# The first two blocks of a fused attention and feed-forward kernel, issued by single steps in a listed order, with attention values gathered by TensorE

## The chip, the cores and the metric

One core of one Trainium2 chip. The time is the device time of one execution in microseconds (us). The kernel before took 239.2 us (median of 3 runs, 238.63 to 239.22). All runs told of here are of one core. Each run also lists its span (from the first to the last instruction) and the mean clock that PE was granted (1.0 is full speed). PE is TensorE, DVE VectorE, ACT ScalarE, POOL GpSimd, SP the engine that only issues transfers.

## The reference, cut to what matters

Chunked attention, then a gated feed-forward layer on its output.

```python
# q, k, v: (4, 8, 768, 64); mem_k, mem_v: (4, 8, 8, 64); chunks of 32 queries
for c in range(24):
    keys   = concat(mem_k, k[l_start:r_end])      # 8 memory rows, 16 left, 32 own, 8 right
    values = concat(mem_v, v[l_start:r_end])
    out[chunk] = softmax(q_c @ keys.T / 8) @ values
x = out as (3072, 512)
return (relu(x @ w_gate) * (x @ w_val)) @ w_out   # 512 -> 1536 -> 512
```

## The kernel before

The 3072 tokens are worked in eight blocks of 384. A block is four windows of 96 queries; eight heads make four head pairs (hp). For a head pair the steps are: turn (bring keys and queries to the layout with 64 dims on partitions), scores, exp, sums (denominators), values, and the product that gives x. A block's feed-forward part is twelve units m, each four matmuls for the gate, four for the value, a relu on ACT and a product on DVE; then three output tiles of twelve matmuls.

From block 2 on, each block's attention runs among the units of the block before it. Blocks 0 and 1 have nothing to hide behind: their order is written out by hand, in whole steps (cut, and short lines joined):

```python
    wide_v(0, 0); wide_d(0, 2); wide_v(0, 1)
    ...                                      # transfers, cut
    ffn_open(0, (0, 1)); wide_v(0, 2); wide_d(0, 3); chunk(0, 0); chunk(0, 1); wide_v(0, 3); chunk(0, 2); chunk(0, 3)
    ffn_close(0)
    ...
    ffn_unit(0, 2, spare=True); ffn_unit(0, 3)
    for hp in range(2):
        turn_pe(1, hp); turn_copy(1, hp)
    step_s(1, 0)                             # scores and exp
    for hp in range(2, HP):
        turn_pe(1, hp); turn_copy(1, hp)
    step_s(1, 1); wide_d(1, 0); ffn_unit(0, 4)   # wide_d: sums, then Ln and Exp
    step_s(1, 2); wide_d(1, 1); ffn_unit(0, 5)
    step_s(1, 3); wide_d(1, 2); ffn_unit(0, 6); wide_d(1, 3); ffn_unit(0, 7)
    one_words(0, ...); ffn_unit(0, 8); ffn_unit(0, 9)
    for hp in range(HP):
        wide_v(1, hp)
    one_words(0, ...); ffn_unit(0, 10); one_words(0, ...); ffn_unit(0, 11); one_words(0, ...)
    load_band(2, v, vwins); load_mem_v(2)
```

The value windows of all blocks come by `load_band`: four transfers a block, in rows of 64 elements. Block 1's units then run in a loop that also clears buffers on DVE, one piece after each of its first six units:

```python
    clear = [lambda: one_words(1, 0, 128, 0, NQ, ONE),
             lambda: (one_words(1, 96, 128, NQ - 1, NQ, 0), one_words(1, 96, 120, NQ - 1, NQ, ONE))]
    clear += [lambda p=p, hh=hh: clear_q(p, hh) for p in range(2) for hh in range(2)]
    ...
            if n == 2 and u < len(clear):    # u: the unit's number
                clear[u]()
```

The softmax here doesn't subtract the row's maximum and nothing guards it: scores larger than these inputs give would overflow.

## Time and profile before

| stretch | us | what limits it |
|---|---|---|
| start to block 1's first unit | 0 to 42.83 | waits among all engines and transfers |
| block 1's units | 42.83 to 63.47 | PE, without a gap |
| the rest | 63.47 to 237.0 | PE, without a gap up to the last output |

This is who PE waited for up to 43 us: writer and line of the waiting group, what ended the wait, us in total, times, longest.

```profile
PE xo_ps L297 <- DVE xT L299: 1.8, 3, 0.7
PE xo_ps L389 <- DVE filler L402: 1.3, 1, 1.3
PE kq_ps L199 <- DMA rq<-in_q_dram: 1.3, 1, 1.3
PE v_ps L342 <- DMA wv<-in_moe_w_val_dram: 0.8, 1, 0.8
PE xs_ps L285 <- ACT rw L288: 0.7, 1, 0.7
PE sc_ps L242 <- DVE kq L216: 0.7, 1, 0.7
PE kq_ps L199 <- POOL sel L429: 0.6, 1, 0.6
PE sc_ps L242 <- ACT ex L273: 0.3, 1, 0.3
```

The second line is the start of the program. The other seven make 6.1 us, and no engine stands out: four name DVE or ACT, two a transfer, one POOL. That is the picture of a start in which every engine hands on to the next. The table by stages and the chain are in the prediction.

### The profile page before, as it was taken

The page shows a single profiled execution, that of the slowest core. Times are in us where ns is not written, and L with a number is a line of the kernel's source. Part 1 is how long each engine was busy: PE and PEld are TensorE (multiplying, and loading weights), DVE is VectorE, ACT ScalarE, POOL GpSimd, SP SyncE. Part 2 cuts the span into 40 slices and gives each one's busy share as a digit, 9 for nine tenths or more (in the row PEclk, how much of TensorE's full clock was granted, in tenths as well). Part 3 has the DMA queues.
Part 4 walks back from the last instruction along what each step waited for, and adds up shares of the span by engine and source line. Part 5 has one row for each costly group of instructions (what it writes and reads, how often), then busy time and mean ns, then how long its engine had stood idle before and what let it go on. Part 6 is the DMA issues. An engine that isn't in the chain of part 4 may idle for free.

```text
span 237.0 us, 4591 instructions
## 1 busy us (share of the span) xinstructions
PE 225.4 (95%) x1730; PEld 131.6 (56%) x1730; DVE 107.4 (45%) x215; ACT 141.0 (59%) x299; POOL 103.8 (44%) x131
## 2 busy tenths in 40 slices
PE   6769888999999999999999999999999999999993
PEld 3535545566544566546664666556654666455641
DVE  5654727889720155604652156405551266214400
ACT  3393593367752589728883599538881798433310
POOL 7978967945306950991079402990040000000000
PEclk9999999999999999999999999999999999999999
DMA  7999999999994999499919998899902100120012
GB/s 120 136 177 194 196 173 184 153 186 161 133 144 178 138 168 173 29 170 163 156 20 145 151 148 87 54 190 150 135 0 89 44 3 0 44 91 0 1 46 89
DMA packets 107324, 27.35 MB, mean 115 GB/s; under 512 B 91222, under 2 KB 104358, under 8 KB 107302
## 3 DMA queue, kind: packets, MB, share of 16 engines
q0 software_dynamic: 83008, 15.37, 82.3%
q1 hardware_dynamic: 20630, 5.33, 19.4%
q10 hardware_dynamic: 3664, 6.36, 7.9%
q8 instruction: 13, 0.21, 0.4%
q14 instruction: 9, 0.07, 0.1%
HBM read 31.15 MB, written 6.29 MB: 158 GB/s over the span
## 4 chain that ended last, share of the span: by engine, by line
PE 85%; DMA 4%; POOL 3%; ACT 3%; DVE 2%; issue 1%; POOLq 0%; DVEq 0%; ACTq 0%
PE g_ps L342 25%; PE v_ps L342 25%; PE o_ps L368 25%; DMA wv<-in_moe_w_val_dram 3%; PE sc_ps L267 3%; PE xo_ps L306 2%; ACT ex L273 2%; PE xs_ps L306 2%; POOL vwin L142 2%; PE kq_ps L199 1%; DMA out_dram<-o_sb 1%; PE sc_ps L242 1%; POOL rk L127 1%; PE gv_ps L342 1%; ACT rw L288 0%
## 5 line engine op out<-in xcount | busy, mean ns | idle before, releaser
L349 DVE TENSOR_TENSOR gv<-v_ps,gr 128x384 f16<-128x384 f32 x95 | 52.8, 557 | 97.4 <-ACT gr L348 84.2
L342 PE MATMUL v_ps<-xT,wv 128*128 128x384 f16 x380 | 78.3, 326 | 0.8 <-DMA wv<-in_moe_w_val_dram 0.8
L342 PE MATMUL g_ps<-xT,wg 128*128 128x384 f16 x380 | 78.3, 326 | 0.0
L368 PE MATMUL o_ps<-wo,gv 128*128 128x512 f16 x288 | 63.5, 379 | 0.0
L348 ACT ACTIVATE gr<-g_ps 128x384 f16<-128x384 f32 x95 | 46.0, 486 | 22.0 <-PE g_ps L342 10.8
L342 PEld LDWEIGHTS <-wg 128*128 128x128 f16 x384 | 36.6, 98 | 22.7
L342 PEld LDWEIGHTS <-wv 128*128 128x128 f16 x384 | 36.2, 98 | 22.8 <-DMA wv<-in_moe_w_val_dram 1.0
L368 PEld LDWEIGHTS <-gv 128*128 128x128 f16 x288 | 28.1, 98 | 32.9
L230 POOL COPY qbd<-qT 64x1536 f16<-64x1536 f16 x10 | 14.6, 1462 | 58.5 <-DMA qT<-q16n 58.2
L377 ACT COPY o_sb<-o_ps 128x512 f32<-128x512 f32 x23 | 13.5, 586 | 39.0 <-PE o_ps L368 31.0
L273 ACT ACTIVATE ex<-sc_ps,bias 128x256 f16<-128x256 f32 x84 | 33.3, 467 | 3.9 <-PE sc_ps L242 3.2
L142 POOL DMA_DIRECT2D vwin<-in_v_dram x32 | 29.0, 934 | 1.7 <-DMA memv<-in_mem_v_dram 1.3
L315 ACT ACTIVATE rinv<-ln,mln 64x768 f32<-64x768 f32 x24 | 22.1, 923 | 0.0
L310 ACT ACTIVATE ln<-xo_ps 64x384 f32<-64x384 f32 x24 | 11.7, 487 | 16.3 <-PE xs_ps L306 16.3
L168 POOL DMA_DIRECT2D q16n<-in_q_dram x20 | 15.6, 805 | 5.5 <-DMA wo<-in_moe_w_out_dram 5.5
L142 POOL DMA_DIRECT2D k<-in_k_dram x20 | 17.9, 909 | 0.0
L321 DVE TENSOR_TENSOR xT<-xo_ps,rinv 64x384 f16<-64x384 f32 x24 | 13.1, 547 | 10.1 <-ACT rinv L315 10.0
L321 DVE TENSOR_TENSOR xT<-xs_ps,rinv 64x384 f16<-64x384 f32 x24 | 13.2, 550 | 0.7
L306 PEld LDWEIGHTS <-vwin 128*128 128x128 f16 x192 | 10.6, 98 | 3.0
L310 ACT ACTIVATE ln<-xs_ps 64x384 f32<-64x384 f32 x24 | 11.4, 474 | 0.0
L306 PE MATMUL xo_ps<-ex,vwin 128*128 128x96 f16 x96 | 11.1, 206 | 0.0
L306 PE MATMUL xs_ps<-ex,vwin 128*128 128x96 f16 x96 | 11.1, 206 | 0.0
(79 smaller groups left out, 134.9 us busy)
## 6 DMA issues: line engine op xcount, KB each, us to landing
out_dram<-o_sb ACTq DMA_DIRECT2D x23, 256.0 KB
vwin<-in_v_dram POOLq DMA_DIRECT2D x24, 120.0 KB, 7.5
q16n<-in_q_dram POOLq DMA_DIRECT2D x20, 96.0 KB, 5.5
k<-in_k_dram POOLq DMA_DIRECT2D x15, 120.0 KB, 4.6
wg<-in_moe_w_gate_dram POOLq DMA_DIRECT2D x6, 256.0 KB, 7.7
wv<-in_moe_w_val_dram POOLq DMA_DIRECT2D x6, 256.0 KB, 8.3
wo<-in_moe_w_out_dram POOLq DMA_DIRECT2D x3, 512.0 KB, 9.7
rk<-in_k_dram POOLq DMA_DIRECT2D x5, 224.0 KB, 7.0
```

What stands on the lines that cost most here:

```text
L142: pool_dma(dsts[p][NMEM + m0:NMEM + m1, i, :, 0:D], src)
L168: pool_dma(q16s[n][:, i], src)
L230: nc.gpsimd.tensor_copy(qbds[n % 2][s, :, :, hh, :].rearrange("p i a m -> p (i a) m"), qTs[n][s].rearrange("p i a m -> p (i a) m"))
L273: nc.scalar.activation(flat[:, :, :, s], view[:, :, :, s], ACT.Exp, scale=SCALE, bias=bias[:, g:g + 1])
L306: nc.tensor.matmul((xo, xs)[hh][:, QB * i:QB * i + QB], lhsT=vw[:, i, 2 * hp + hh, :], rhs=ex[:, hh, i, :], start=True, stop=True)
L310: nc.scalar.activation(ln[:, hh], (xo, xs)[hh][D:128], ACT.Ln, scale=1.0 / 64.0)
L315: nc.scalar.activation(rinv, lns.pop((n, hp)), ACT.Exp, scale=-1.0, bias=mln64[0:D, :])
L321: nc.vector.tensor_tensor(out=x_of(n)[D * hh:D * hh + D, hp, :], in0=(xo, xs)[hh][0:D], in1=rinv[:, hh, :], op=ALU.mult)
L342: nc.tensor.matmul(ps[a], lhsT=(wg, wv)[a][:, f, 128 * m:128 * m + 128], rhs=xTs[n][:, f, :], start=(f == 0), stop=(f == NFC - 1))
L348: nc.scalar.activation(gr, g_ps, ACT.Relu)
L349: nc.vector.tensor_tensor(out=gvs[n][:, m, :], in0=v_ps, in1=gr, op=ALU.mult)
L368: nc.tensor.matmul(o_ps, lhsT=gvs[n][:, m, 128 * t:128 * t + 128], rhs=wo[:, m, :], start=(m == 0), stop=(m == NDC - 1))
```

## The change

Its intent: cut PE's waits before block 1. Three parts, in the words of its author: blocks 0 and 1 by single steps in an order found with a model of the engines, values gathered by TensorE, block 2's memory values sent while block 0's units run.

The order is now a list of short names (T turn, S scores, e exp, D sums, L and E the Ln and the Exp of the denominators, G gather of values, cg its copy, V values, m product, g and v the halves of a unit, r its relu, mu its product):

```diff
-    ffn_unit(0, 2, spare=True)
-    ffn_unit(0, 3)
-    for hp in range(2):
-        turn_pe(1, hp)
-        turn_copy(1, hp)
-    step_s(1, 0)
...
+    go("""
+        Vb1 mb0 Vb3 Vb2 mb1 ch0 Eb3 ch1 mb2 mb3 ch2 ch3 r0 r1 g2 v2 mu0 r2 T0 mu1 g3 cq0 v3 ck0 T2 r3 mu2 mu3
+    """)
+    zero(vwins[0][0:NMEM + 16, 0, :, 0:D], 0.0)
+    load_mem_v(2)
+    go("""
+        cq2 ck2 T1 ck1 S0 g4 e0 cq1 v4 r4 S1 D0 mu4 T3 e1 L0 g6 S2 e2 v6 ck3 D1 cq3 r6 E0 g5 mu6 L1 r5 S3 v5 g7
+        v7 mu5 e3 r7 g9 mu7 E1 D2 G0 r9 g8 v9 L2 cg0 mu9 v8 G1 D3 cg1 E2 r8 g11 V0 v11 L3 r11 mu8 m0 V1 g10 m1
+        V2 m2 V3 E3 m3 v10 mu11 r10 mu10
+    """)
```

The values of blocks 0 and 1 come in rows of 256 elements and are spread to windows by a selection matrix on PE; the key order inside a window changes with it (masks and biases too):

```diff
-    load_band(0, v, vwins)
+    load_rows_mem(pool_dma, rv[KR:KR + 2], 0, 0, H, mem_v)
+    load_v_rows(0)
...
+    def gather_v(n, g, pool, tag):
+        ps = vgs[n, g] = pool.tile([128, 2, 512], F32, tag=tag, name="vg_ps").rearrange("p a (i c) -> p (a i) c", i=2)
+        for i in range(NQ):
+            for j in range(J):
+                nc.tensor.matmul(ps[32 * j:32 * j + 32, i].rearrange("p (h d) -> p h d", d=D),
+                                 lhsT=sels[n][0:KR + 2, i, :], rhs=rv[:, 4 * g:4 * g + 4, D * j:D * j + D],
+                                 start=True, stop=True)
```

And three pieces of clearing move into the loop of block 1's units:

```diff
-    one_words(0, 0, 128, 0, 1, ONE)
...
-    clear = [lambda: one_words(1, 0, 128, 0, NQ, ONE),
+    clear = [window0_ones, lambda: one_words(0, 0, 128, 1, 2, ONE), lambda: one_words(0, 0, 128, 2, NQ, ONE),
+             lambda: one_words(1, 0, 128, 0, NQ, ONE),
```

The diff holds more than the three parts name. Block 0's rows of keys and queries come sooner: those of heads 2 and 3 move from POOL's queue to those of SP and ACT, and POOL issues those of heads 4 to 7 first. There are 14 filler matmuls at the start instead of 10.

## The prediction

> **What bounds the kernel now.** I first read the stretches by stage (engine busy time between times that I took from the timeline of TensorE, PE): before the first turn, block 0's attention, its first two feed-forward units, units 2 and 3, block 1's turns and first scores, the rest of block 1 beside units 4 to 9, the last values and units 10 and 11, block 1's units, the first outputs, and one later block. Columns: length, busy us (instructions) of PE, weight loads, DVE, ACT, POOL, then PE's clock, busy DMA, GB/s.
> ```profile
> 0.00:5.20 5.20, 3.38 (x10) 1.37 (x11) 2.58 (x23) 1.65 (x2) 3.93 (x12) 1.00 0.67 124
> 5.20:16.60 11.40, 8.96 (x145) 5.97 (x145) 7.06 (x12) 6.72 (x12) 11.19 (x17) 1.00 1.54 148
> 16.60:20.65 4.05, 3.29 (x27) 1.70 (x26) 1.11 (x2) 1.44 (x4) 2.25 (x6) 1.00 1.46 193
> 20.65:23.34 2.69, 2.69 (x17) 1.47 (x16) 2.11 (x5) 1.56 (x4) 2.69 (x5) 1.00 1.45 195
> 23.34:27.46 4.12, 3.14 (x85) 2.57 (x85) 3.94 (x8) 1.39 (x4) 4.12 (x6) 1.00 1.46 199
> 27.46:38.20 10.74, 9.83 (x80) 5.47 (x76) 3.85 (x8) 9.69 (x23) 8.05 (x12) 1.00 1.77 176
> 38.20:42.83 4.63, 3.80 (x49) 2.47 (x49) 3.86 (x9) 0.94 (x2) 3.56 (x4) 1.00 1.56 177
> 42.83:63.19 20.36, 20.36 (x210) 12.15 (x209) 17.45 (x32) 12.97 (x30) 12.58 (x16) 1.00 1.81 163
> 63.19:79.50 16.31, 16.31 (x90) 7.70 (x90) 2.84 (x6) 6.50 (x13) 6.61 (x7) 1.00 1.10 146
> 79.50:105.57 26.07, 26.07 (x183) 15.60 (x180) 11.09 (x20) 18.02 (x39) 17.46 (x20) 1.00 1.50 137
> ```
> From 42.83 us, where block 1's units begin, PE is busy without a gap; every later block is PE alone, 26.07 us each. The change rewrites only what lies before 42.83. So the question is one number: **when does block 1's first unit start?** Everything after should shift with it.
>
> Second, the chain that ended last. In 5 to 43 us it names the wait for the first value weights, then PE, then ACT:
> ```profile
> 10.20 7.43 DMA wv<-in_moe_w_val_dram
> 29.89 1.09 ACT ex L273 x3
> 32.39 1.09 ACT ex L273 x3
> ```
> Third, ACT's timeline in that stretch, for the real spacing of its work:
> ```profile
> 28.90 0.61 ACT L289 ACTIVATE rw<-rw,mln 128x384 f32<-128x384 f32 x1
> 29.42 0.47 ACT L348 ACTIVATE gr<-g_ps 128x384 f16<-128x384 f32 x1
> 29.79 1.20 ACT L273 ACTIVATE ex<-sc_ps,bias 128x256 f16<-128x256 f32 x3
> 30.86 0.51 ACT L288 ACTIVATE rw<-xs_ps 128x384 f32<-128x384 f32 x1
> 31.40 0.61 ACT L289 ACTIVATE rw<-rw,mln 128x384 f32<-128x384 f32 x1
> ```
> The starts say what an instruction costs in a full queue, less than its duration: three exps 1.07, Ln 0.54 (the Exp needs its result), Exp 0.52, relu 0.37. ACT is full from 28 to 36 us, 2.5 us per head pair, each with only one unit on PE: that pins PE.
>
> **What the Trainium skill says.** "TensorEngine Tiling (Array Packing)", Tiling Modes: weights of 32 columns make four independent tiles of the array, of 64 columns two; a change of mode drains the array. The trace agrees for two: eight value matmuls of 96 columns (64 weight columns) started at 38.21 and the next group at 38.41, 25 ns each against 96/2.4 = 40 ns alone; a run of feed-forward matmuls after attention work costs 0.76 instead of 0.65 us. Four tiles are in no row of this trace. "DMA: Bandwidth & Descriptors", Why small descriptors are slow: a 256-byte descriptor pays a fixed part. The trace agrees: 138 to 139 GB/s at 8 to 12 us, with the value windows (rows of 64 elements) in the queue, 194 to 197 at 18 to 28 with weights and 1 KB rows. "TensorE: Matmul & The Clock Gate", Part 1: PE starts at half clock, freed after some 3.4 us of work. The trace agrees: the fillers start 0.32 us apart, as 384 columns at 1.2 GHz would; later ones of that width 0.163. "VectorE: DVE Perf Modes", Why PSUM operands drop a tier: fp32 from PSUM at the basic rate; 896 columns took 1092 ns, 512 took 679, so 1024 should take about 1.23 us.
>
> **The change part by part.**
>
> *Values by row gathers.* Out: eight window loads of 112 to 120 KB (0.91 us of POOL each, 7.3 in all), eight copies of memory values (four of 0.43 on DVE, four of 0.60 on POOL). In: for each of two blocks, rows in 448 KB by two transfers, two gathers of 16 matmuls (32 weight columns, 256 wide) and two 1.23 us copies on DVE. A gather costs 16*256/2.4 = 1.7 us one after another, 0.43 packed by four; with drains I take 0.55. So +2.2 us of PE in all, +4.9 of DVE. I choose packed because the twofold case is seen here.
>
> *First weights.* The first wv is issued at 10.20 behind four window loads and lands at 17.63; PE waits 0.8 for it. Now its issue stands after eight POOL transfers that start at some 2.2 us, so about 7.2 to 8. Ahead of it: 0.83 MB of fp32 rows on the two hardware queues and 1.39 MB (rows, values, weights) at some 194 GB/s: landing 12.5 to 14. PE asks at about 15.8. This wait goes.
>
> *Rows of heads 4 to 7 of block 0.* The queries held PE 1.26 us (10.05). They are issued at some 3 instead of 5.1 and should be there at 8 to 9, when they are asked for. Gone.
>
> *Fillers and validity.* 14 fillers instead of 10 and nine small matmuls: the first turn may start at 5.5 instead of 5.2, +0.3.
>
> *Block 0, walked by hand* with these spacings (turn 0.30 + 0.45, since keys are now written in runs of 32; mask 0.42, scores 0.28, sums 0.29, values 0.20, gather 0.55; exp 0.81; 0.2 from a matmul to its reader): first turn 5.5; scores 0 at 7.8; third turn 8.6; sums 0 at 10.5; gathers 11.1 and 13.0; the copy of the second done at 14.95; x of pair 0 at 15.4; first chunk 15.75; x of pair 3 at 16.95; two units done at 18.35 instead of 20.65. **Gain 2.3 us**; about 1.1 is the weights' wait, the rest is order.
>
> *From there to block 1's first unit.* PE has 10 units of 1.30 (13.0), turns 4*0.42, scores 4*0.28, sums 4*0.29, values 4*0.25, gathers 2*0.55: 19.1. Before, the same less gathers (18.0) took 42.83 - 20.65 = 22.2, so 4.2 were waits. Order now: turns spread between units 2 to 4, scores 0 at 23.0 (was 25.19), one or two half units between two scores, Ln parted from Exp so that neither waits for the other, values and four half units at the end. My walk leaves 2.1 of waits: 0.8 before unit 4, where DVE is full with copies of turns (ck 0.60, cq 0.46, mult 0.47 by starts), and the rest by unit 8 and the last values (DVE: gather copies). So 18.35 + 19.1 + 2.1 = 39.55. **Block 1 starts 3.3 us sooner.**
>
> *Block 1's units.* Three groups of ones move from DVE before 42.83 into the first three units (3*0.27 + 0.27 + 0.48 = 1.6 us), and the clearing runs to the ninth unit. DVE is busy 17.45 of 20.36 there, and its products lag: the one for the v at 51.95 (ended 52.76) starts at 54.60 and ends at 55.16, and the unit two later wants that bank at 55.90: 0.74 of slack. I book 0.3 of new PE waits, and 0.3 for what the walk has missed. Memory values sent sooner are worth nothing: block 2's first use is at 50.3, and PE doesn't wait there.
>
> Sum: -3.3 + 0.3 + 0.3 = -2.7; 239.2 - 2.7 = **236.5 us**.
>
> **The rivals.**
> *Weights become the bound.* From wv at 17.63 to the landing of wg of columns 1024 on at 31.3 (POOL waited for it), 2.4 MB came: the 194 GB/s. From a landing of t the new order gives units 4 and 5 their weights at t + 9.7, 6 and 7 at t + 12.4, 8 and 9 at t + 17.4. With t = 12.5 that is 22.2, 24.9, 29.9 against asks at 23.75, 26.2, 31.4: 1.3 to 1.5 of slack. With t = 16 PE waits 2 us and the result is 238.5. For it: DMA is near its rate throughout. Against: the slow window loads are gone.
> *Gathers run one after another.* +1.15 us of PE each, four of them, part beside waits: about +3, so 239 to 239.5, no gain.
> *DVE becomes the bound.* It loses 1.7 and gets 4.9 us of copies before 42.83, and most waits of my walk end on it. If each step is 0.1 slower than in my walk, +1.5: 238.
> *The order fits perfectly.* No waits from 18.35 on: 37.5, and 234.1. That, and a quicker block 0, is the only way past 2% (234.4), since PE's own work is then the floor.
>
> **Range and chances.** 234.0 is the perfect order; 239.0 is one rival in full. More than 2% faster needs nearly all of the 2.1 us of waits to vanish: 0.15. Slower by 2% needs two rivals at once: 0.03.
>
> **What would show it.** Block 1's first unit at about 39.5 (was 42.83) and the same time from there to the end (wrong if that grows by over 0.5: DVE in block 1's units). The first chunk at about 15.8, with no wait for wv (wrong: a wait for wv, or for the value rows rv at the first gather). A gather of 16 matmuls in about 0.5 us (wrong: 1.7). ACT no longer full for 8 us on end; DVE as the main releaser of PE between 18 and 39. PE's waits for wg and wv in units 4 to 11 near zero.

## The result, and the profile after

The changed kernel took **236.41 us** (median of 4 runs, 236.2 to 237.37) against 239.21 (4 runs): ratio 0.9895, 95% interval 0.9864 to 0.9927. Two later sessions, with the changed kernel unaltered as a control, gave 236.65 against 238.53 (0.9926, 0.9906 to 0.9946) and 236.97 against 238.48 (0.9936, 0.9915 to 0.9958). A ratio is the mean time of one kernel's runs over that of the other's of the same rounds, so not quite the ratio of the medians. The mean of the three ratios is 0.992: some 1.9 us. A fourth session, between these two, ran other versions without this control.

Some of that lies where no view of the profile looks. The time exceeded the span by 1.66 to 1.76 us in all 16 runs of the changed kernel, and by 1.89 to 1.99 in the 33 runs of the kernel before in the three later sessions. So about 0.24 us of the gain is outside the span; its cause stays open.

The two pages' head lines say little; PE is busy 227.0 us instead of 225.4, as it has the gathers to do:

```profile
span 235.7 us, 4736 instructions
PE 227.0 (96%) x1807; PEld 131.2 (56%) x1807; DVE 109.9 (47%) x214; ACT 141.0 (60%) x300; POOL 96.6 (41%) x124
```

The changed kernel by stages, in the columns of the prediction's table: block 0's attention from the first turn, its first two units, from there to block 1's first scores, from there to block 1's first unit, block 1's units, the first outputs.

```profile
5.20:16.30 11.10, 9.22 (x190) 5.88 (x190) 7.48 (x12) 7.45 (x14) 9.21 (x18) 1.00 1.40 181
16.30:18.91 2.61, 2.61 (x19) 1.58 (x17) 1.35 (x3) 1.01 (x3) 1.86 (x3) 1.00 1.45 194
18.91:23.71 4.80, 4.42 (x66) 2.71 (x65) 3.65 (x8) 1.57 (x4) 2.97 (x5) 1.00 1.46 197
23.71:40.72 17.01, 16.39 (x196) 8.79 (x193) 10.53 (x18) 11.89 (x28) 10.47 (x15) 1.00 1.50 182
40.72:62.25 21.53, 20.77 (x218) 12.34 (x216) 19.05 (x39) 13.49 (x30) 12.21 (x15) 1.00 1.76 169
62.25:77.90 15.65, 15.65 (x83) 7.31 (x80) 2.80 (x6) 6.04 (x12) 11.63 (x13) 1.00 1.32 155
```

Block 1's first unit starts at 40.72 instead of 42.83 (-2.11). But block 1's units now take 21.53 us instead of 20.64 (63.47 - 42.83), and PE is not busy all of that time. So the first output comes only 1.22 us sooner (62.25 against 63.47), and the span is 1.3 shorter. This is who PE waited for from 5 to 62 us:

```profile
PE sc_ps L263 <- DVE kq L229: 0.7, 1, 0.7
PE kq_ps L207 <- DMA rk<-in_mem_k_dram: 0.6, 1, 0.6
PE kq_ps L207 <- DVE rk L536: 0.6, 1, 0.6
PE v_ps L380 <- DMA wv<-in_moe_w_val_dram: 0.5, 1, 0.5
PE xs_ps L316 <- ACT rw L321: 0.4, 1, 0.4
PE q_ps L207 <- DMA rq<-in_q_dram: 0.4, 1, 0.4
PE sc_ps L263 <- DVE kq L232: 0.2, 1, 0.2
```

The first line is the wait in block 1's units; the other six, 2.7 us, stand where 6.1 stood before. So 3.4 us of waits went, and four gathers of 0.55 us came in their place (2.2): 1.2 of the 2.1. The remaining 0.9 lies before unit 2, and the timelines account for it: block 0's turns of keys and queries, waits taken out, took PE 4.0 us before and take 2.8 now. The matmuls of the keys took 0.39 us a head pair from 11.40 us on before, 0.22 at 9.57 now, as the keys of a window are written in runs of 32 (0.42 in the mended run of the old transfers below, which keeps the old key order).

Three questions for experiments. What is the wait for DVE at 56 us, and does it cost time? Are the waits for transfers (0.6, 0.5, 0.4) chance, or has the transfer of weights become a second bound? And which part of the change earns the gain?

### The profile page after: what moved, and what is told of

The parts are those of the page before. It is cut to its first block, busy times and chain, and to the rows that moved or that the text cites. A ratio compares the mean times of both kernels' runs of the same rounds, so it can differ in the third digit from the quotient of the medians.

```text
span 235.7 us, 4736 instructions
## 1 busy us (share of the span) xinstructions
PE 227.0 (96%) x1807; PEld 131.2 (56%) x1807; DVE 109.9 (47%) x214; ACT 141.0 (60%) x300; POOL 96.6 (41%) x124
## 4 chain that ended last, share of the span: by engine, by line
PE 84%; DMA 11%; DVE 2%; issue 1%; ACT 0%; POOL 0%; POOLq 0%
PE o_ps L416 25%; PE g_ps L380 25%; PE v_ps L380 25%; DMA wv<-in_moe_w_val_dram 4%; DMA wg<-in_moe_w_gate_dram 3%; DMA rk<-in_k_dram 3%; PE sc_ps L287 3%; PE xo_ps L344 2%; PE xs_ps L344 2%; DMA out_dram<-o_sb 1%; PE sc_ps L263 1%; PE kq_ps L207 1%; DVE gv L392 1%; DVE qbd L659 1%; DVE kq L222 1%
## 5 line engine op out<-in xcount | busy, mean ns | idle before, releaser
L388 ACT ACTIVATE gr<-g_ps 128x384 f16<-128x384 f32 x95 | 46.1, 487 | 19.1 <-PE g_ps L380 10.3
L145 POOL DMA_DIRECT2D vwin<-in_v_dram x24 | 21.7, 929 | 2.0 <-DVE gv L392 1.3
```

The costliest lines, as they stand in the source:

```text
L145: pool_dma(dsts[p][NMEM + m0:NMEM + m1, i, :, 0:D], src)
L388: nc.scalar.activation(grs[n, m], g_ps, ACT.Relu)
```

## The experiments

### The control: the changed kernel again

> The changed kernel once more, unaltered, as the control. Both theories: 236.4 us (236.2 to 236.6), 2.8 below the kernel before. The profiled execution of the first time took 237.4 while its timed ones took 236.2 to 236.5; if the 0.5 us wait for the value weights of units 4 and 5 and the 0.7 us wait for DVE at 56 us are chance of that one execution, this trace lacks one of them; if they belong to the kernel, both are here again and block 1's units again take 21.5 us from the first to the first output (20.6 in the kernel before).

Measured: 236.65 us (6 runs), ratio 0.9926. Both waits are in the trace again (0.48 for the value weights of unit 4, 0.66 for DVE at 56.7 us), and block 1's units took 21.53. Both belong to the kernel. The profiled execution was again the slowest of its session (237.5).

### Clearing moved out of block 1's units

```diff
+    CLEAR_AT = (0, 1, 2, 16, 17, 14, 15, 12, 13)
-            if n == 2 and u < len(clear):
-                clear[u]()
+            if n == 2 and u in CLEAR_AT:
+                clear[CLEAR_AT.index(u)]()
```

> The changed kernel, with six of the nine clearing steps on DVE (ones of the second window, zeros of the spread queries) moved from block 1's units 3 to 8 into the output units after them, where DVE is nearly idle; the three that the change moved here stay in units 0 to 2. Theory (clears crowd DVE in block 1's units and hold PE): the stretch from block 1's first unit to the first output falls from 21.5 to 20.6 us, no wait for DVE at 56 us, and the time falls by 0.6 to 0.9 us to 235.6. Rival (the wait is of that one profiled execution alone, or another wait takes its place): 236.4, within 0.3 of the changed kernel.

Measured: 235.73 us, ratio 0.9885 beside 0.9926 of the control in the same session; 0.9885/0.9926 is 0.9959, so 1.0 us less. First the changed kernel's timeline around the wait (start, duration, engine, line; cut to DVE and the waiting matmuls):

```profile
53.29 0.70 DVE L659 MEMSET qbd<- 64x768 uint32 x1
...
54.62 0.70 DVE L659 MEMSET qbd<- 64x768 uint32 x1 [0.22 <-issue]
...
55.34 0.69 DVE L222 CAST kq<-kq_ps 128x512 f16<-128x512 f32 x1
...
55.95 0.55 DVE L229 CAST kq<-kq_ps 128x384 f16<-128x384 f32 x1
...
56.56 0.34 PE L263 MATMUL sc_ps<-kq 64*128 64x96 f16 x8 [0.66 <-DVE kq L229]
```

The turn's matmuls were issued from 52.92 to 53.43, but DVE comes to copy their result only at 55.34, after two clearings of 0.70 us and a product. The scores wait for the copy. The same place with the clearing moved, then the whole stretch:

```profile
52.64 0.69 DVE L222 CAST kq<-kq_ps 128x512 f16<-128x512 f32 x1 [0.23 <-PE kq_ps L207]
...
53.24 0.55 DVE L229 CAST kq<-kq_ps 128x384 f16<-128x384 f32 x1
...
54.92 0.34 PE L263 MATMUL sc_ps<-kq 64*128 64x96 f16 x8
```

```profile
39.81:60.44 20.63, 20.63 (x218) 12.35 (x216) 15.65 (x32) 13.20 (x30) 12.46 (x15) 1.00 1.77 160
```

Now DVE waits for PE (0.23) and the scores for nobody; block 1's units take 20.63 us, as before the change, and DVE is busy 15.65 of it instead of 19.05. So the change gave back 0.9 us in block 1's units. The three clearings that it moved there push the six that were there already on to units 3 to 8, among the copies; with the six out of the way the wait is gone, so the cause is shown. A second session:

> clears_late again, beside mixed_clears and the changed kernel on one chip: 0.9 us below the changed kernel if the crowding of DVE is the whole effect, 235.6 to 235.8.

Measured: 236.06 us, ratio 0.9898 beside 0.9936 of its control: 0.9962, 0.9 us less, and 20.63 for the stretch.

### Fewer rows ahead of the weights (wrong result)

```diff
-        turn_mms(rows_of(n)[0], steps, ..., hp)
+        turn_mms(rows_of(n)[0], steps, ..., hp % 2 if n == 1 else hp)
...
     load_rows(1, 0, 4)
-    load_rows(1, 4, 4)
```

> The changed kernel without the load of block 1's rows of heads 4 to 7 (0.42 MB of writes ahead of the weights of units 4 and 5); the turns of these heads take heads 0 to 3 instead, so the result is wrong on purpose. Rival theory (transfers have become a co-bound before block 1): the waits for query rows (0.4) and for the value weights (0.5) go, weights of units 4 to 11 land some 2 us sooner, block 1's first unit starts about 1 us sooner (39.7 instead of 40.7) and the time falls by 0.8 to 1.0. Theory (PE's order and DVE/ACT set the start, the waits for transfers are soaked up by later ones): under 0.3 us faster.

Measured: 236.23 us, ratio 0.9903 beside 0.9926 of the control (0.9977, 0.5 us less), between the two expectations; the intervals of the two overlap. (Its outputs still passed the comparison with the reference: queries and keys are drawn so small that the softmax is nearly flat, and swapped heads hardly show. It computes something else all the same.) The trace is clearer. From unit 2 on (19.20) to block 1's first unit (40.17):

```profile
19.20:40.17 20.97, 20.70 (x258) 11.72 (x256) 14.04 (x25) 13.47 (x32) 14.64 (x21) 1.00 1.59 184
```

The same stretch took 21.81 in the first trace of the changed kernel and 22.08 in the control. All waits for transfers in it are gone (0.20 us for DVE is left). Its start was no sooner, as the casts of the first keys waited longer in that execution.

### The new order with the old transfers

```diff
-    load_rows_mem(pool_dma, rv[KR:KR + 2], 0, 0, H, mem_v)
-    load_v_rows(0)
+    load_band(0, v, vwins)
...
-    load_v_rows(1)
+    for i in range(NQ):
+        nc.gpsimd.tensor_copy(vwins[1][0:NMEM, i, :, 0:D], mem16)
+    load_band(1, v, vwins)
```

with the old key order, masks and memory copies, and the steps G, cg, Gb and cgb taken out of the lists.

> The new order of steps with the old way of the values: windows by the slow transfers, memory values by copies, old key order, no gathers. Theory (the quicker transfers are needed, as the new order asks for weights sooner): the first chunk waits for the first value weights until 17.3 to 17.6 us again, block 1's first unit starts at 41.5 to 42.3 (40.7 with the whole change), and the time is 237.5 to 238.3. Rival (the order carries the gain, and the gathers cost 2.2 us of PE which this kernel saves): 236.4 or less.

Measured: 237.01 us (0.9938, 0.9908 to 0.9968). This run had a flaw of mine: on DVE the cast of the memory values stood ahead of the key casts and waited for its transfer until 6.84 us, so the first turn started at 7.65 instead of 5.2. The median also lies between two groups: 237.85 and 237.55 us at a mean clock of 0.993, and 236.48 and 236.27 at 0.999 and 1.0. The trace is of the first. In it the clock was 0.62 from 8 to 10 us and 0.53 from 10 to 12, just after PE had waited 2.09 us for the cast, and 1.00 from there on; all 13 other traces show 1.00 from 8 to 12 us. So the runs at full clock are at the rival's 236.4, and the median does not speak against it. What lowered the clock was not tested.

The run is still of use. With everything 2.4 us late the transfers were all in time, and from unit 2 (21.31) to block 1's first unit (40.97) it took 19.66 us. Beside the 20.97 without waits above, block 1's two gathers and their copies cost 1.3 us of this stretch (one trace each; the key order differs too).

Mended, the cast after the key casts:

> As order_alone, without its flaw: the cast of the memory values stood ahead of block 0's key casts on DVE and held the first turn until 7.65 us; here it comes after them. Theory A (the gathers cost 2.2 us of PE and more of DVE, which is more than the quick value transfers give back): the first turn at 5.3, the first chunk's value weights at 17.3 to 17.7 with a wait for them, unit 2 at about 20.1, block 1's first unit at 39.7 to 40.2 (40.7 to 40.9 in the changed kernel), and the time 0.5 to 0.9 us below the changed kernel: 235.7 to 236.1. Theory B (the new order needs the quick transfers): waits for weights of units 4 to 9 come back, block 1's first unit at 40.7 or later, time 236.5 or more.

Measured: 236.67 us, ratio 0.9927 (0.9893 to 0.9961): about the same as the whole change (0.9926 in the session before). The comparison is across sessions and chips: no run of the changed kernel was made beside this one, and one of the 11 runs of the kernel before that were made beside it took 240.67 us at a clock of 0.993, which widens the interval to 0.8 us either way. Neither theory fits whole. Block 1's first unit came at 39.97, as theory A says, but the first chunk did not wait for its weights: it began at 16.29, not at 17.6. My placing of the first weights behind the window loads in time was wrong for this order of issue. PE waited 0.6 us for gate weights, 0.5 for DVE and three times for ACT (1.3 us) instead. So of the two main parts the order, with the sooner rows of block 0, carries most of the gain. Whether the gathers as a whole pay is not shown: the spans of this run are shorter against the kernel before than those of the changed kernel (1.84 us in the mean beside 1.55 and 1.36), but its times exceed its spans by 2.05 us instead of 1.70.

With the clearing moved as well:

> order_alone2 with the six clearing steps moved as in clears_late. Both theories have block 1's units at 20.6 us again, so 0.9 below order_alone2: theory A 234.8 to 235.2, below clears_late (235.7); theory B 235.6 or more.

Measured: 236.48 us, ratio 0.9917 (0.9881 to 0.9952). The stretch of block 1's units was 20.64, as expected, but block 1 started at 40.56, 0.6 later than in the run above, with a wait of 0.44 for query rows that the other lacked. The 0.9 did not show in the time: the gain of 0.2 is inside the noise. The spans are 0.6 shorter in the mean (234.08 beside 234.68), but two of the six runs took 3.24 and 3.02 us beyond their spans instead of 2.0 to 2.1. In the one trace late transfers take 0.6 back; that they do so in the timed runs is not shown.

### Gathers for block 0 only, with the clearing moved

From the kernel with the clearing moved: block 1's values by the slow transfers and memory copies, its key order as of old.

```diff
-        steps = kps.rearrange("p (i j t) -> p j i t", i=NQ, j=J) if n < 2 else ...
+        steps = kps.rearrange("p (i j t) -> p j i t", i=NQ, j=J) if n == 0 else ...
-    load_v_rows(1)
+    for i in range(NQ):
+        nc.gpsimd.tensor_copy(vwins[1][0:NMEM, i, :, 0:D], mem16)
+    load_band(1, v, vwins)
```

> Clears late; values by gathers for block 0 only, block 1's windows by the slow transfers and memory copies. Theory A with the part of B that holds for the first weights (quick transfers pay before the first chunk, not after): first chunk at 16.0 to 16.3 without a wait for weights, and from unit 2 to block 1's first unit 19.7 to 20.2 (21.2 in clears_late), so block 1 at 38.6 to 39.2 and 234.5 to 235.0. Rival (transfers bound this stretch, the slow windows put the weights of units 8 to 11 behind): no gain over clears_late, 235.7.

Measured: 235.37 us, ratio 0.9876 (0.9842 to 0.9910), below both kernels. Block 1 started at 39.33; from unit 2 it took 20.74, not 19.7 to 20.2, with two waits for value weights (0.52 and 0.27). It was run beside the version above, differs from it by block 0's values and key order alone, and took 1.1 us less (235.37 and 236.48). But the intervals overlap, and the spans differ by only 0.3 in the mean (233.82 and 234.08). So that gathers pay in block 0 is likely, not shown. A second session, beside the others on one chip:

> mixed_clears again beside clears_late: 0.3 to 0.5 us below it if gathers pay only in block 0; equal to it if the first difference (235.37 in one call, 235.73 in another) was between chips.

Measured: 235.79 us, ratio 0.9886; clears_late 0.9898 and the changed kernel 0.9936 in that session. It is the fastest in both, 1.2 us below the changed kernel (0.9886/0.9936 is 0.9950), 0.3 below clears_late; that last difference is within the intervals (0.9865 to 0.9907 and 0.9877 to 0.9919), so it is likely, not shown.

### Each gather twice

```diff
-        for i in range(NQ):
+        for i in [*range(NQ)] * 2:
```

> The changed kernel with each gather of 16 matmuls issued twice (same result): 4 x 0.55 = 2.2 us more PE work. If PE's own work sets the time before block 1: 1.5 to 2.2 us slower, 237.9 to 238.6. If PE mostly waits for others there (transfers, DVE, ACT), so that gathers hide in waits: under 0.7 slower.

Measured: 238.25 us, ratio 0.9992 (0.9942 to 1.0041), 0.7% above the mean of the changed kernel's three: some 1.7 us, for 64 matmuls (across sessions, 1.2 us either way). The trace fits: PE was busy 21.72 us from unit 2 to block 1's first unit, where the changed kernel's first trace has 20.81, so 0.9 for block 1's two gathers. Gathers are not hidden in waits. The timeline gives their price; first the changed kernel, then this one, each with the group that follows:

```profile
11.80 0.62 PE L527 MATMUL vg_ps<-rv,sel 114*32 114x256 f16 x16
...
12.35 0.36 PE L316 MATMUL xs_ps<-ex,ones 128*64 128x96 f16 x4
```

```profile
11.23 1.06 PE L527 MATMUL vg_ps<-rv,sel 114*32 114x256 f16 x32
12.22 0.36 PE L316 MATMUL xs_ps<-ex,ones 128*64 128x96 f16 x4
```

Sixteen took 12.35 - 11.80 = 0.55 us until the next group began, 32 took 0.99. So sixteen more cost 0.44. Full-width matmuls of 384 columns start 0.163 us apart in these traces; at that pace 16 of 256 columns would take 1.74 us in turn, nearly 4 times as much. So the four tiles of 32 columns do run side by side. The first sixteen cost 0.11 more, which I take for the change of mode; nothing here separates it from other fixed costs.

### Block 2's memory values sent late, as before

```diff
-    load_mem_v(2)
     go("""
...
     load_band(2, v, vwins)
+    load_mem_v(2)
```

> The changed kernel with the third part undone: block 2's memory values are sent after block 0's units again, not among them. Theory (they were never waited for, block 2's first values are used at 48 us): no difference, within 0.3 us of the changed kernel of this call, no wait of PE for them. Rival (the small transfers now collide with the window loads issued at the same time and hold block 2's values): 0.5 us or more slower, with a wait of PE for the memory values near 48 us.

> The changed kernel as it is, the control of this call: 236.4 to 236.7, and again 21.5 us from block 1's first unit to the first output.

Measured: 237.04 us (0.9941) and 236.97 (0.9936): no difference, as expected. SP issues these transfers at 36.05 us in the one and 36.60 in the changed kernel's first trace: moving them up the program did not make them start sooner, so the third part of the change does nothing for the time.

The pair told more than was asked. The late sending comes after 36 us, and yet the two traces differ from 18 to 41. First mem_late, from unit 2 to block 1's first unit and its units; then the control:

```profile
18.61:39.58 20.97, 20.77 (x259) 11.64 (x257) 14.04 (x25) 13.45 (x32) 12.95 (x18) 1.00 1.51 190
39.58:61.10 21.52, 20.76 (x218) 12.35 (x216) 19.04 (x39) 13.49 (x30) 12.54 (x16) 1.00 1.76 162
```

```profile
18.55:40.93 22.38, 20.89 (x257) 11.51 (x256) 14.19 (x25) 13.47 (x32) 13.91 (x20) 1.00 1.48 183
```

In mem_late's execution every transfer came in time: 20.97 us, the same as with fewer rows. In the control's, PE waited for key rows (0.47), query rows (0.26) and gate weights (0.30), then for DVE (0.47): 22.38. The profiled times were 236.25 and 237.57. All timed runs of the changed kernel lie between 236.2 and 237.57. So with this order one and the same kernel has executions in which the transfers hold PE and others in which they do not, and that makes about 1.3 us. It fits that the timed runs near 236.2 are of the second kind; they have no trace, so this is not shown.

## Why the prediction was right

It said 236.5 us, and 236.41 came; over three sessions the gain was nearer 1.9 us than the 2.7 forecast. By its steps:

- **Everything is decided before block 1's first unit, and the rest shifts with it.** Right for the rest: from the first output on the two spans end 1.2 to 1.3 apart, as they enter it.
- **Block 0 done at 18.35.** Four traces with the changed order show 18.55 to 18.91. The first chunk came at 15.9 to 16.3 (15.75 forecast), and its weights were there. The walk missed that the second head pair's key rows, now on a hardware queue, come late: PE waited for their cast 0.2 to 0.6 us.
- **A gather costs 0.55 us.** 0.55, packed by four, as chosen. The rival of gathers one after another is out.
- **From there 21.2 us to block 1's first unit.** The sum came right by luck: both of its terms are wrong. It counted 19.1 us of PE's work and 2.1 of waits. In the trace of mem_late the profile lists no wait of PE from 18.61 to 39.58, and the stretch still took 20.97. So PE's own work, as it is spaced, is 20.97 us, and the waits for DVE did not come. The slip stands already in the reading of the kernel before: 4.2 of 22.2 us were put down to waits, but those that the profile lists between 20.65 and 42.83 make 2.4. Part of what is missing is the 0.76 instead of 0.65 us of a half unit beside attention work, which the prediction read and left out of its sum. So the rival of a perfect order (37.5) was out of reach: 18.35 + 20.97 is 39.3. The other traces took 21.81 to 22.38 (three of the changed kernel) and 21.19 and 21.60 (the two of clears_late, whose order is the same there).
- **Weights at t + 9.7, with 1.3 us to spare.** This step failed: "units 4 and 5 their weights at t + 9.7 ... 22.2 ... against asks at 23.75". What was mis-sized is mainly t, the landing of the first value weights. The sum took 12.5, the low end of its own 12.5 to 14 (at 14 the first slack is 0.05); they landed at 14.7 in the first trace and at 14.0 to 16.0 in the other three. The value weights of unit 4 came 9.6 to 10.8 after them, at 25.45 in the first trace, and PE waited 0.5 us for them. The rival "weights become the bound" was called and given too little: it holds in three of the four traces with the changed order, and costs 0.8 to 1.4 us there. "PE's waits for wg and wv in units 4 to 11 near zero" is wrong with it.
- **DVE as the main releaser of PE between 18 and 39.** Wrong: in that stretch PE waited for transfers, or for nobody. Of the versions with all gathers, only two have a wait there that names DVE: 0.47 in the control of the last session and 0.20 with fewer rows.
- **Block 1's units: 0.3 of new waits.** The mechanism was named rightly, DVE's lag under the clearing that moves there, and mis-sized: 0.9 us in every trace. The sum looked at the bank that the next products need (0.74 of slack). What broke first was another reader of DVE: the copies of block 2's third turn.
- **ACT no longer full for 8 us on end.** Wrong: ACT was busy 7.87 of the 8 us from 28 to 36 before, and 7.76 of those from 27 to 35 in the first trace after (7.76 of 26 to 34 in mem_late's). But PE was busy 7.09 of these 8 us before and all 8.00 after. So a full ACT does not by itself pin PE; in the new order PE had half units to do while ACT worked.
- **Memory values sent sooner are worth nothing.** Right.

So the sum -3.3 + 0.3 + 0.3 reads, by the trace of the first session, -2.1 + 0.9 = -1.2; by one with the transfers in time, 39.58 - 42.83 = -3.25 and +0.9, so -2.4. The timed runs, at -1.5 to -2.8, lie about there, with 0.24 of them outside the span. The mechanism was right in the main: the new order takes out most of PE's waits before block 1's first unit. That the forecast fell so close is partly luck: too little work and too many waits cancelled, late transfers cost 0.8 to 1.4 us in most traces, DVE's lag 0.6 more than booked, and the first session was the kindest of the three to it.

## What to carry to other kernels

When you take waits out of a stretch, write down for each queue how much it has to spare afterwards: here PE's order and the transfers of weights had so little between them that of the 1.3 us of PE work that leaving out block 1's gathers frees, 0.45 to 0.67 arrived (20.74 us from unit 2 to block 1 against 21.19 in the first run of clears_late, 20.93 against 21.60 in the second; single traces, whose spread is as large). Work that is "off the path" (clearing a buffer) still stands in an engine's queue ahead of something that is on it; put it where that engine is idle, here in the output units, which was worth 0.9 us for three lines. When you walk an order by hand, add up the waits that the profile lists before you call the rest work: here the walk's total was right and both of its terms were wrong by some 2 us. And try the parts of a change alone: the order, with the sooner rows, carried most of the gain, what the gathers brought is within the noise, and the third part did nothing.

## What the Trainium skill lacked or had wrong

- "TensorEngine Tiling (Array Packing)" gives the gain of 32-column tiles as "Up to 4×" (Theoretical Speedup) and says that a change of mode drains the array (Key Properties), without a time. The runs with 16 and 32 matmuls show nearly 4 for weights of 114 rows by 32 columns and 256 columns moving (0.44 us for what would take 1.74 in turn), and at most 0.11 us for the change of mode (0.55 against 0.44).
- "DMA: Bandwidth & Descriptors", Bandwidth, has no rate for a transfer that casts fp32 to fp16. Here the traces show 194 to 197 GB/s moved in the stretches full of weights and rows. The sizes that they list are those written (256 KB for 128 x 4 x 256 weights of fp16), so by my estimate twice that was read.
- No page that I used says how much the landing of the same transfers differs between executions of one kernel: the stretch from unit 2 to block 1 took 20.97 us with all of them in time and up to 22.38 with waits for them.
